# Converting weights through a PSUM bank on VectorE, and placing the second batch's key sums over several blocks

## The chip, the cores and the metric

The kernel runs on one core of a Trainium2 chip. The core has five engines with a queue each: TensorE (PE, matmuls; its weight loads are shown as PEld), VectorE (DVE), ScalarE (ACT), GpSimd (POOL) and SyncE (SP, which issues the DMAs). The metric is the device time of one execution in microseconds: 2738.78 us before the change, the median of three runs (2738.58 to 2742.02).

## The reference

Inputs are q (2 batches of 12288 rows of 128), kv (2 x 384 x 32 x 128), a 128 x 128 projection w_sr, and two pairs of feed-forward weights, 128 x 2048 and 2048 x 128, all float32.

```python
kv_pool = kv.reshape(B, H // 4, 4, W // 4, 4, C).mean(axis=(2, 4))
k = v = kv_pool.reshape(B, -1, C) @ w_sr          # 768 keys a batch
a = softmax(q @ k.T / sqrt(C));  x = a @ v
h = x @ w_in1;  x = (h * clip(h + 3, 0, 6) / 6) @ w_out1
h = x @ w_in2;  out = (h * cos(h)) @ w_out2
```

## The kernel before

**Tiling.** The 24576 rows are cut into 48 blocks of 512, 24 to a batch. A block goes through attention (transposed q, four score tiles of 128 rows by 768 keys, row maximum, exponential, normalisation, transposition of the weights, product with the values) and then through layer 1 and layer 2 in 8 units each. A unit is six matmuls into a pair of PSUM banks (`ff_in`, lines 762 to 764), ScalarE and VectorE work on the pair (lines 777 and 780 in layer 1; 785, 788, 794 and 797 in layer 2), a split of the result into a high and a low part (ScalarE line 824, GpSimd line 800) and six matmuls into an accumulating bank (`ff_out`, lines 770 to 772). Every product is made of three matmuls with operands split into a high and a low part, so the weights have to be split too. Layer 2 runs 15 units behind layer 1.

**Key sums.** `plan_kv` averages 16 rows of kv into a key. A batch has six chunks; a chunk is loaded into two `w` tiles and added up by halves on VectorE (line 445): 1024 elements of one tile to the other, then 512, 256 and 128 within the tile. The first batch stops after two such additions and lets PE finish (`KV_HALVINGS`), the second makes all four. PE transposes the sum (line 454), `mean` copies it into the tile `pt` (line 467), and `project` makes keys and values of it (lines 515, 519, 497, 500).

**Weights.** `plan_weight` converts the 16 parts of the four weight matrices (512 words of 8 bytes a partition each). Its steps use the loaded tile `raw` and a second `w` tile of two halves: `magnitude` (ACT, line 352), `clamp`, `rebase`, `sign` (DVE, lines 357, 364, 371), `high` (ACT, line 390), `power`, `rest` (DVE, lines 378, 385), `low` and `add` (POOL, lines 394, 398). PE may use a part when its last step is done.

**Order.** `Plan.run` writes the order of all engines when the program is built. It is a list scheduler: an operation has a priority in nanoseconds, a cost on the engines that can do it (`where`), operations that it follows, and slots that it takes and gives back (13 `w` tiles, 8 PSUM banks taken singly or as adjacent pairs, and others). Nothing whose priority lies more than `WINDOW` = 100000 above that of the first unfinished operation may begin. `KV_AHEAD` and `KV_PROJECT` say by how much the priority of a batch's key sums and of its projection lies before that of its first block, and the step (2000) how far the six chunks lie apart. On the chip each engine then takes its list strictly in order, and waits where an input or a buffer is not ready.

**PSUM.** Scores, transposed attention weights and each unit's `ff_in` take a pair of the 8 banks; each layer's accumulator, the attention product and small transposes take a single one.

## Time and profile before

| | |
|---|---|
| median of the runs | 2738.78 us |
| profiled execution | 2738.04 us, of which the span is 2736.2 us |
| PE busy | 2649.4 us (97%), 11504 instructions |
| ACT busy | 2308.1 us (84%) |
| DVE busy | 2123.9 us (78%) |
| POOL busy | 2057.3 us (75%) |
| granted PE clock | 0.99 of full speed as a mean |

The busy shares are means over the whole span. The kernel has three regimes: a start, in which keys and weights are prepared; a long stretch in which one block follows the other; and, near 1160 to 1400 us, the change from the first batch to the second. The profile's view by stretches and the timeline show them apart. PE busy means that a matmul is under way, not that PE runs at its full rate, so the time from one block to the next is the better measure of what PE loses.

### The profile page before, as it was taken

The numbers are of one execution on the slowest core, as the hardware profiler recorded it, in microseconds if no ns is written. First come the engines' busy times: TensorE is split into PE (matmuls) and PEld (weight loads), VectorE is DVE, ScalarE is ACT, GpSimd is POOL, SyncE is SP. The second block draws the span as 40 slices with busy tenths as digits, with TensorE's granted clock in tenths as the row PEclk, the third lists the DMA queues.
The fourth block names the chain that finished last, engine by engine and source line by source line (L and its number), as shares of the span: only waits on it lengthen the run. The fifth ranks groups of instructions, "written<-read, shape, count | busy, mean of one in ns | idle before, by whom it ended". The sixth has DMA issues, their size and how long they took to land. (4 is left out here: it accounts for less than half of the span.)

```text
span 2736.2 us, 32247 instructions
## 1 busy us (share of the span) xinstructions
PE 2649.4 (97%) x11504; PEld 2108.1 (77%) x11504; DVE 2123.9 (78%) x2224; ACT 2308.1 (84%) x2647; POOL 2057.3 (75%) x999
## 2 busy tenths in 40 slices
PE   6789999999999999988999999999999999999999
PEld 5567788878877887766788788878877887888787
DVE  6887777777787787788787777877877777778776
ACT  3578888889898888877788898988888888888888
POOL 3786778777777877767687787778777878787777
PEclk9999999999999999999999999999999999999999
DMA  5123222322232232323223222322332232223210
GB/s 174 46 76 82 67 59 71 84 62 55 72 83 62 55 85 70 101 76 85 55 77 77 58 58 72 83 62 55 79 76 62 60 86 68 58 64 90 55 51 12
DMA packets 387058, 193.00 MB, mean 71 GB/s; under 512 B 292561, under 2 KB 367441, under 8 KB 386897
## 3 DMA queue, kind: packets, MB, share of 16 engines
q1 hardware_dynamic: 386896, 190.95, 26.8%
q8 instruction: 90, 1.47, 0.2%
q14 instruction: 72, 0.58, 0.1%
HBM read 33.62 MB, written 84.93 MB: 43 GB/s over the span
## 5 line engine op out<-in xcount | busy, mean ns | idle before, releaser
L800 POOL TENSOR_TENSOR lo<-w,hi 128x1024 fp32r<-128x1024 f32 x768 | 1838.0, 2417 | 609.5 <-ACT hi L824 393.6
L824 ACT CAST hi<-w 128x1024 fp32r<-128x1024 f32 x768 | 786.7, 1056 | 158.9 <-DVE w L780 106.7
L762 PE MATMUL banks<-x,w_in_hi 128*128 128x512 f32 x1536 | 640.0, 417 | 28.1 <-DVE w L780 15.0
L797 DVE TENSOR_TENSOR w<-w,banks 128x1024 f32<-128x1024 f32 x384 | 463.6, 1218 | 206.6 <-ACT w L794 206.5
L770 PE MATMUL banks<-hi,w_out_hi 128*128 128x512 f32 x1536 | 607.4, 395 | 0.0
L764 PE MATMUL banks<-x,w_in_hi 128*128 128x512 f32 x1536 | 603.1, 393 | 1.2 <-DVE x L734 1.2
L763 PE MATMUL banks<-x,w_in_lo 128*128 128x512 f32 x1536 | 602.9, 392 | 0.0
L772 PE MATMUL banks<-lo,w_out_hi 128*128 128x512 f32 x1536 | 600.6, 391 | 1.6 <-POOL lo L800 1.6
L771 PE MATMUL banks<-hi,w_out_lo 128*128 128x512 f32 x1536 | 599.7, 390 | 0.0
L780 DVE SCALAR_TENSOR_TENSOR w<-w,banks 128x1024 f32<-128x1024 f32 x384 | 457.3, 1215 | 138.9 <-ACT w L777 138.8
L788 DVE SCALAR_TENSOR_TENSOR w<-banks,w 128x1024 f32<-128x1024 f32 x384 | 463.7, 1218 | 58.5 <-ACT w L785 56.4
L777 ACT ACTIVATE w<-banks,three 128x1024 f32<-128x1024 f32 x384 | 417.6, 1115 | 57.5 <-PE banks L764 55.0
L794 ACT ACTIVATE w<-w 128x1024 f32<-128x1024 f32 x384 | 404.5, 1067 | 32.8 <-DVE w L788 30.0
L785 ACT ACTIVATE w<-banks 128x1024 int32<-128x1024 f32 x384 | 388.7, 1026 | 49.1 <-PE banks L764 48.2
L762 PEld LDWEIGHTS banks<-x,w_in_hi 128*128 128x128 f32 x1536 | 290.4, 189 | 125.9 <-DVE w L780 27.8
L763 PEld LDWEIGHTS banks<-x,w_in_lo 128*128 128x128 f32 x1536 | 290.6, 189 | 71.4 <-issue 16.5
L764 PEld LDWEIGHTS banks<-x,w_in_hi 128*128 128x128 f32 x1536 | 290.2, 189 | 64.2 <-DVE x L734 1.9
L772 PEld LDWEIGHTS banks<-lo,w_out_hi 128*128 128x128 f32 x1536 | 288.8, 188 | 64.2 <-POOL lo L800 3.1
L771 PEld LDWEIGHTS banks<-hi,w_out_lo 128*128 128x128 f32 x1536 | 289.4, 188 | 60.4 <-issue 2.4
L770 PEld LDWEIGHTS banks<-hi,w_out_hi 128*128 128x128 f32 x1536 | 289.6, 189 | 59.7 <-issue 1.7
L652 DVE COPY w<-w 128x1536 uint16<-128x1536 uint16 x184 | 317.2, 1744 | 1.4 <-POOL w L624 1.1
L711 PE MATMUL banks<-w,v_all 128*128 128x512 f32 x576 | 272.1, 596 | 4.4 <-ACT w L322 2.5
(64 smaller groups left out, 1970.2 us busy)
## 6 DMA issues: line engine op xcount, KB each, us to landing
scr<-w SPq DMA_DIRECT2D x184, 384.0 KB, 2.5
w<-in_kv_dram SPq DMA_DIRECT2D x48, 256.0 KB, 5.9
w<-in_q_dram SPq DMA_DIRECT2D x48, 256.0 KB, 2.8
out_dram<-w SPq DMA_DIRECT2D x48, 256.0 KB, 2.0
w<-in_moe_w_in_dram SPq DMA_DIRECT2D x8, 512.0 KB, 5.4
w<-in_moe_w_out_dram SPq DMA_DIRECT2D x8, 512.0 KB, 4.0
w<-scr SPq DMA_TRANSPOSE x138, 4.6
w_sr_sb<-in_w_sr_dram SPq DMA_DIRECT2D x1, 64.0 KB, 2.0
```

The costliest lines, as they stand in the source:

```text
L762: nc.tensor.matmul(t[:, i, :], w_hi[:, k, :], xx[:, 0, :], start=True, stop=False)
L763: nc.tensor.matmul(t[:, i, :], w_lo[:, k, :], xx[:, 0, :], start=False, stop=False)
L764: nc.tensor.matmul(t[:, i, :], w_hi[:, k, :], xx[:, 1, :], start=False, stop=True)
L770: nc.tensor.matmul(t, o_hi[:, k, :], h[:, i, :], start=(k == 0), stop=False)
L771: nc.tensor.matmul(t, o_lo[:, k, :], h[:, i, :], start=False, stop=False)
L772: nc.tensor.matmul(t, o_hi[:, k, :], l[:, i, :], start=False, stop=(k == 2 * NP - 1))
L777: nc.scalar.activation(plan[g], two(ps), AF.Relu, bias=three, scale=1.0)
L780: nc.vector.scalar_tensor_tensor(out=plan[g], in0=plan[g], scalar=6.0, in1=two(ps), op0=ALU.min, op1=ALU.mult)
L788: nc.vector.scalar_tensor_tensor(out=plan[g], in0=two(ps), scalar=0.25, in1=plan[g].bitcast(I32), op0=ALU.add, op1=ALU.subtract,)
L797: nc.vector.tensor_tensor(out=plan[g], in0=plan[g], in1=two(ps), op=ALU.mult)
L800: nc.gpsimd.tensor_tensor(out=plan[lo], in0=plan[g], in1=plan[hi].bitcast(F32), op=ALU.subtract)
L824: prio + HI_AT, {"act": 947}, lambda e: nc.scalar.copy(plan[hi], plan[g]), [a],
```

## The change

In `plan_weight` the second work tile becomes one PSUM bank (`one(tt)`), and a new slot `turn`, of which there is one, lets one part be converted at a time. The two GpSimd steps go to VectorE: `add` now comes before `low` and adds the rest to the rounded word in PSUM, and `low` subtracts the high part from it. `sign` writes in place into `raw`. A part has seven VectorE instructions in place of five, all with a PSUM operand, and no GpSimd instruction: 112 instead of 80 on VectorE, 32 fewer on GpSimd. The costs that the planner is told change with that. For the key sums `KV_AHEAD` becomes 200000 for both batches; the second batch's chunks lie 25000 apart instead of 2000; `KV_PROJECT` becomes 10000; and the planner is told 1.6 ns for an element of the second batch's additions instead of 1.04.

```diff
--- before.py
+++ after.py
@@ -41,6 +41,8 @@
 BY_PE = 2
 
 NBANKS = 8
+
+TURNS = 1
 ET_SPARE = 2
 
 W_SPARE = 3
@@ -49,7 +51,7 @@
 
 WINDOW = 100000.0
 LOAD_AHEAD = 5000
-KV_AHEAD, KV_PROJECT = 60000, 4000
+KV_AHEAD, KV_STEP, KV_PROJECT = 200000, 25000, 10000
 KV_HALVINGS = 2
 WARM = 3
 A_STEP = 2000
@@ -293,6 +295,7 @@
             "lo": tiles("lo", NLO, [P, 2, T], F32R),
             "x": tiles("x", NX, [P, 2, T], F32R),
             "s": tiles("s", 8, [P, 4], F32),
+            "turn": list(range(TURNS)),
             "one": free_banks,
             "two": free_banks,
             "scr": tiles("scr", NSCR, [NKC // 2, NJ * P * 2, 2 * P], U16, dram),
@@ -340,8 +343,8 @@
             return r[:, :, 0].bitcast(U32), r[:, :, 1]
 
         def work():
-            t = plan[tt].bitcast(I32)
-            return t[:, 0, :], t[:, 1, :]
+
+            return one(tt).bitcast(I32)
 
         def load(e):
             nc.sync.dma_start(
@@ -349,64 +352,64 @@
             )
 
         def magnitude(e):
-            nc.scalar.activation(work()[0].bitcast(F32), words()[1].bitcast(F32), AF.Abs)
+            nc.scalar.activation(work().bitcast(F32), words()[1].bitcast(F32), AF.Abs)
 
         def clamp(e):
 
-            t32 = work()[0].bitcast(F32)
+            t32 = work().bitcast(F32)
             nc.vector.tensor_scalar(
                 out=t32, in0=t32, scalar1=SMALLEST, scalar2=None, op0=ALU.max
             )
 
         def rebase(e):
 
-            t = work()[0]
+            t = work()
             nc.vector.tensor_scalar(
                 out=t, in0=t, scalar1=3, scalar2=0x3FFFFFF8,
                 op0=ALU.logical_shift_left, op1=ALU.bitwise_and,
             )
 
         def sign(e):
-            t, top = work()
+            top = words()[1]
             nc.vector.scalar_tensor_tensor(
-                out=top, in0=words()[1], scalar=-(1 << 30), in1=t,
+                out=top, in0=top, scalar=-(1 << 30), in1=work(),
                 op0=ALU.bitwise_and, op1=ALU.bitwise_or,
             )
 
         def power(e):
-            t, top = work()
             nc.vector.tensor_scalar(
-                out=t, in0=top, scalar1=-(1 << 23), scalar2=None, op0=ALU.bitwise_and
+                out=work(), in0=words()[1], scalar1=-(1 << 23), scalar2=None, op0=ALU.bitwise_and
             )
 
         def rest(e):
 
-            t32 = work()[0].bitcast(F32)
+            t32 = work().bitcast(F32)
             nc.vector.scalar_tensor_tensor(
                 out=t32, in0=words()[0], scalar=2.0**-52, in1=t32, op0=ALU.mult, op1=ALU.mult
             )
 
         def high(e):
-            nc.scalar.copy(hi, work()[1].bitcast(F32))
+            nc.scalar.copy(hi, words()[1].bitcast(F32))
+
+        def add(e):
+            t32 = work().bitcast(F32)
+            nc.vector.tensor_tensor(out=t32, in0=t32, in1=words()[1].bitcast(F32), op=ALU.add)
 
         def low(e):
-            top32 = work()[1].bitcast(F32)
-            nc.gpsimd.tensor_tensor(out=top32, in0=top32, in1=hi.bitcast(F32), op=ALU.subtract)
-
-        def add(e):
-            t, top = work()
-            nc.gpsimd.tensor_tensor(out=lo, in0=top.bitcast(F32), in1=t.bitcast(F32), op=ALU.add)
+            nc.vector.tensor_tensor(
+                out=lo, in0=work().bitcast(F32), in1=hi.bitcast(F32), op=ALU.subtract
+            )
 
         a = op(prio, {"dma": 1560}, load, take=[(raw, "w")], spare=W_SPARE)
-        a = op(prio, {"act": 520}, magnitude, [a], take=[(tt, "w")])
-        a = op(prio, {"dve": 335}, clamp, [a])
-        a = op(prio, {"dve": 335}, rebase, [a])
+        a = op(prio, {"act": 560}, magnitude, [a], take=[(tt, "one"), (("turn", n, part), "turn")])
+        a = op(prio, {"dve": 602}, clamp, [a])
+        a = op(prio, {"dve": 602}, rebase, [a])
         c = op(prio, {"dve": 602}, sign, [a])
         a = op(prio, {"act": 520}, high, [c])
-        c = op(prio, {"dve": 335}, power, [c])
-        a = op(prio, {"pool": 1225}, low, [a, c])
-        c = op(prio, {"dve": 602}, rest, [c], drop=[raw])
-        a = op(prio, {"pool": 1225}, add, [a, c], drop=[tt])
+        c = op(prio, {"dve": 602}, power, [c])
+        c = op(prio, {"dve": 602}, rest, [c])
+        c = op(prio, {"dve": 602}, add, [c, a], drop=[raw])
+        a = op(prio, {"dve": 602}, low, [c], drop=[tt, ("turn", n, part)])
         for k in range(part * WK, (part + 1) * WK):
             w_ready[n, k] = a
 
@@ -472,7 +475,7 @@
             a = [load(0), load(1)]
             for n in range(halvings):
                 w = 1024 >> n
-                where = {"dve": 70 + 1.04 * w}
+                where = {"dve": 70 + (1.6 if b else 1.04) * w}
                 if n == 0:
                     where["pool"] = 2303
                 a = [op(prio, where, add(n), a, drop=[] if n else [keys[1]])]
@@ -893,7 +896,8 @@
     projects = {}
 
     def pool_kv(prio, batch):
-        projects[batch] = plan_kv(prio, batch, 2000, *((4, 0) if batch else (KV_HALVINGS, WARM)))
+        step, *how = (KV_STEP, 4, 0) if batch else (2000, KV_HALVINGS, WARM)
+        projects[batch] = plan_kv(prio, batch, step, *how)
 
     def project_kv(prio, batch):
         for h in range(2):
```

In the changed kernel's rows below, lines above 410 stand 3 higher than before (L445 is L448, L454 is L457, L515 is L518).

PE's queue at the start, the first batch's keys, before. L454 transposes a chunk's sum, L462 is filler, L515 and L519 are the projection of one half, L555 transposes a block's q:

```order
L454 MATMUL banks<-ident,w_82 128x128 x4
L462 MATMUL banks<-ident 128x128 x3
L515 MATMUL banks<-w_84,w_sr_sb 128x384
L519 MATMUL banks<-w_sr_sb,w_84 128x128 x3
L454 MATMUL banks<-ident,w_85 128x128 x4
L462 MATMUL banks<-ident 128x128 x3
L454 MATMUL banks<-ident,w_87 128x128 x4
L462 MATMUL banks<-ident 128x128 x3
L555 MATMUL banks<-ident,w_79 128x128 x4
L454 MATMUL banks<-ident,w_89 128x128 x4
L555 MATMUL banks<-ident,w_78 128x128 x4
```

and in the changed kernel:

```order
L457 MATMUL banks<-ident,w_82 128x128 x4
L465 MATMUL banks<-ident 128x128 x3
L457 MATMUL banks<-ident,w_85 128x128 x4
L465 MATMUL banks<-ident 128x128 x3
L457 MATMUL banks<-ident,w_87 128x128 x4
L465 MATMUL banks<-ident 128x128 x3
L457 MATMUL banks<-ident,w_89 128x128 x4
L465 MATMUL banks<-ident 128x128 x3
L518 MATMUL banks<-w_84,w_sr_sb 128x384
L522 MATMUL banks<-w_sr_sb,w_84 128x128 x3
L518 MATMUL banks<-w_84,w_sr_sb 128x384
L522 MATMUL banks<-w_sr_sb,w_84 128x128 x3
```

The projection of the first half stood after the third chunk; both halves now stand after the sixth, and both transposes of q after them.

ScalarE's queue a little later, before: L352 is `magnitude`, L390 `high`, L609 the exponential, L322 the copy of transposed attention weights:

```order
L352 ACTIVATE w_85<-w_80 128x512
L497 ACTIVATE v_all<-banks 128x384
L352 ACTIVATE w_87<-w_83 128x512
L390 CAST w_in_hi<-w_82 128x512
L352 ACTIVATE w_79<-w_86 128x512
L609 ACTIVATE w_89,s_110<-banks,s_110 128x768
L609 ACTIVATE w_78,s_111<-banks,s_111 128x768
L352 ACTIVATE w_84<-w_88 128x512
L609 ACTIVATE w_81,s_112<-banks,s_112 128x768
L352 ACTIVATE w_82<-w_90 128x512
L390 CAST w_in_hi<-w_85 128x512
```

and in the changed kernel (L355, L392, L612, L325), where L730 is the copy that makes the first block's input of layer 1:

```order
L392 CAST w_in_hi<-w_81 128x512
L612 ACTIVATE w_84,s_114<-banks,s_114 128x768
L612 ACTIVATE w_79,s_115<-banks,s_115 128x768
L325 COPY w_78<-banks 128x1024
L355 ACTIVATE banks<-w_80 128x512
L325 COPY w_81<-banks 128x1024
L325 COPY w_86<-banks 128x1024
L612 ACTIVATE w_88,s_116<-banks,s_116 128x768
L392 CAST w_in_hi<-w_80 128x512
L612 ACTIVATE w_90,s_117<-banks,s_117 128x768
L355 ACTIVATE banks<-w_83 128x512
L730 CAST x_106<-banks 128x512
```

Where several `magnitude` ran ahead, each now writes a bank, `banks`, and comes after the part before it has been finished; one of them stands right ahead of L730.

VectorE's queue where the second batch's key sums begin, before (L445 the additions, L780 the gate of layer 1, L603 the row maximum):

```order
L780 SCALAR_TENSOR_TENSOR w_90<-w_90,banks 128x1024
L445 TENSOR_TENSOR w_79<-w_79,w_80 128x1024
L445 TENSOR_TENSOR w_78<-w_78,w_82 128x1024
L445 TENSOR_TENSOR w_79<-w_79 128x512
L780 SCALAR_TENSOR_TENSOR w_83<-w_83,banks 128x1024
L780 SCALAR_TENSOR_TENSOR w_87<-w_87,banks 128x1024
L780 SCALAR_TENSOR_TENSOR w_88<-w_88,banks 128x1024
L603 TENSOR_REDUCE s_114<-banks 128x1
L603 TENSOR_REDUCE s_115<-banks 128x1
L445 TENSOR_TENSOR w_79<-w_79 128x256
L603 TENSOR_REDUCE s_116<-banks 128x1
L445 TENSOR_TENSOR w_79<-w_79 128x128
```

and in the changed kernel (L448, L783, L800, L791, L564):

```order
L737 TENSOR_TENSOR x_109<-banks,x_109 128x512
L448 TENSOR_TENSOR w_90<-w_90,w_81 128x1024
L564 TENSOR_TENSOR x_104<-banks,x_104 128x512
L791 SCALAR_TENSOR_TENSOR w_82<-banks,w_82 128x1024
L448 TENSOR_TENSOR w_90<-w_90 128x512
L783 SCALAR_TENSOR_TENSOR w_78<-w_78,banks 128x1024
L800 TENSOR_TENSOR w_82<-w_82,banks 128x1024
L783 SCALAR_TENSOR_TENSOR w_88<-w_88,banks 128x1024
L448 TENSOR_TENSOR w_90<-w_90 128x256
L448 TENSOR_TENSOR w_90<-w_90 128x128
L783 SCALAR_TENSOR_TENSOR w_85<-w_85,banks 128x1024
```

The additions of two chunks stood back to back; now those of a chunk stand between the work of units, and the first two chunks begin some 100 rows earlier in VectorE's queue. 22 of the 24 additions remain on VectorE; two first additions (1024 elements) are now in GpSimd's queue.

## Rows read from the trace of the kernel before

**Rows 1.** Stretches of the span: length, busy us of each engine (instructions), PE clock, DMA.
```profile
30.00:60.00 30.00, 19.32 (x86) 15.72 (x85) 29.61 (x50) 17.72 (x33) 19.49 (x16) 0.85 0.23 78
...
60.00:110.00 50.00, 38.34 (x142) 25.54 (x141) 35.48 (x42) 29.96 (x36) 35.43 (x21) 0.92 0.28 84
...
110.00:160.00 50.00, 36.44 (x144) 27.95 (x143) 49.83 (x52) 28.88 (x37) 36.45 (x20) 0.93 0.29 74
...
148.00:284.00 136.00, 124.90 (x516) 96.02 (x516) 107.39 (x109) 110.14 (x126) 102.70 (x52) 0.97 0.30 73
...
400.00:600.00 200.00, 200.00 (x883) 161.66 (x882) 155.68 (x165) 176.61 (x202) 154.48 (x75) 1.00 0.29 72
...
1160.00:1240.00 80.00, 64.36 (x256) 50.78 (x256) 72.15 (x63) 54.25 (x61) 53.65 (x24) 0.88 0.29 75
```

**Rows 2.** ScalarE's timeline: start, us; the layer-2 input cast, once per block.
```profile
389.62 0.61 ACT L729 ACTIVATE x<-banks 128x512 fp32r<-128x512 f32 x1
...
1145.39 0.61 ACT L729 ACTIVATE x<-banks 128x512 fp32r<-128x512 f32 x1
...
1725.06 0.63 ACT L729 ACTIVATE x<-banks 128x512 fp32r<-128x512 f32 x1
```

**Rows 3.** Timeline where the second batch's key sums begin: start, us, [idle before <-releaser].
```profile
1159.38 9.03 POOL L800 TENSOR_TENSOR lo<-w,hi 128x1024 fp32r<-128x1024 f32 x3 [4.08 <-ACT hi L824]
...
1159.79 6.42 DVE L445 TENSOR_TENSOR w<-w,w 128x1024 f32<-128x1024 f32 x2
...
1166.14 2.82 DVE L445 TENSOR_TENSOR w<-w 128x512 f32<-128x512 f32 x1
...
1170.15 1.01 PE L597 MATMUL banks<-k_hi,x 128*128 128x384 f32 x2 [5.39 <-DVE w L780]
```

**Rows 4.** VectorE's groups, 1150 to 1360 us: the second batch's key sums by shape.
```profile
L445 DVE TENSOR_TENSOR w<-w,w 128x1024 f32<-128x1024 f32 x6 | 13.4, 2253 | 0.0
L445 DVE TENSOR_TENSOR w<-w 128x512 f32<-128x512 f32 x6 | 11.1, 1847 | 0.1
L445 DVE TENSOR_TENSOR w<-w 128x256 f32<-128x256 f32 x6 | 9.0, 1508 | 0.0
L445 DVE TENSOR_TENSOR w<-w 128x128 f32<-128x128 f32 x6 | 7.7, 1276 | 0.1
```

**Rows 5.** The page's groups kept apart by shape: weight conversion on VectorE, whole span.
```profile
L385 DVE SCALAR_TENSOR_TENSOR w<-w,w 128x512 f32<-128x512 uint32 x16 | 22.4, 1400 | 0.1
L357 DVE TENSOR_SCALAR w<-w 128x512 f32<-128x512 f32 x16 | 17.4, 1091 | 4.3 <-ACT w L352 4.3
L371 DVE SCALAR_TENSOR_TENSOR w<-w,w 128x512 int32<-128x512 int32 x16 | 15.2, 953 | 0.2 <-PE banks L764 0.2
L364 DVE TENSOR_SCALAR w<-w 128x512 int32<-128x512 int32 x16 | 14.7, 922 | 0.1
L378 DVE TENSOR_SCALAR w<-w 128x512 int32<-128x512 int32 x16 | 10.8, 676 | 0.1
```

**Rows 6.** Single lines of the weight conversion: ns min/median/max.
```profile
L357 DVE TENSOR_SCALAR w<-w x16: 406/428/2601, 30.8 to 165.7; 128x512 f32<-128x512 f32 x16
...
L385 DVE SCALAR_TENSOR_TENSOR w<-w,w x16: 673/1752/2253, 35.4 to 173.4; 128x512 f32<-128x512 uint32 x16
```

**Rows 7.** Groups by shape: VectorE's tensor_scalar of 512 elements that reads PSUM.
```profile
L849 DVE TENSOR_SCALAR w<-banks 128x512 f32<-128x512 f32 x42 | 28.6, 682 | 1.0 <-PE banks L772 0.9
```

**Rows 8.** Timeline of the start: first batch's projection, first scores, first layer-2 unit.
```profile
30.00 0.81 PE L515 MATMUL banks<-w,w_sr_sb 128*128 128x384 f32 x2
30.65 0.83 PE L519 MATMUL banks<-w_sr_sb,w 128*128 128x128 f32 x6
31.23 0.42 PE L597 MATMUL banks<-k_hi,x 128*128 128x384 f32 x1
...
148.25 1.21 DVE L788 SCALAR_TENSOR_TENSOR w<-banks,w 128x1024 f32<-128x1024 f32 x1
```

**Rows 9.** SyncE's issues of the second batch's key loads: ns min/median/max.
```profile
L433 SPq DMA_DIRECT2D w<-in_kv_dram x24: 536/565/600, 1149.9 to 1275.4; - x24
```

## The prediction

> **What bounds the kernel now.** I read the view by stretches first, then the timeline of one instruction that comes once per block, then the timeline where that period breaks. Between 400 and 600 us PE is busy for 200.00 of 200 us at full clock while VectorE has 155.68, or 78% [rows 1]: there only PE's own work counts. The layer-2 input cast comes once per block, 48 times in all. From 389.62 to 1145.39 lie 14 periods, 53.98 us each; the ten from 1145.39 to 1725.06 take 579.67 us, where ten full-rate periods would take 539.8 [rows 2]. So the change of batch costs 39.9 us, and in the first 80 us of it (1160 to 1240) PE is busy 64.36 us at a granted clock of 0.88, and VectorE 72.15 [rows 1]. Why is seen in the timeline: three additions stand in a row on VectorE from 1159.79 to 1168.96, 9.2 us, beside a GpSimd that works without a gap; the gate behind them is late, and PE waits 5.39 us for its bank [rows 3]. PE had thus about 3.8 us of work in hand. The four shapes of addition average 2.25, 1.85, 1.51 and 1.28 us, with little fall for an eighth of the elements [rows 4]: much of it is waiting for GpSimd.
>
> The other loss is the start. VectorE is busy 29.61 of 30 us to 60, 35.48 of 50 to 110, 49.83 of 50 to 160, and PE falls behind [rows 1]. There the 80 conversion instructions take 22.4 + 17.4 + 15.2 + 14.7 + 10.8 = 80.5 us, 1.006 us each [rows 5], though the same shapes take 0.406 or 0.673 us at best [rows 6]: 48 x 0.406 + 32 x 0.673 = 41.0 us is work, 39.5 us is waiting. Two things are therefore worth time: VectorE's at the start and in the middle. GpSimd's relief is worth only what it takes from VectorE.
>
> **The start.** Each part has seven VectorE steps for five, 112 for 80. None has two inputs in SBUF, and all touch PSUM. The nearest row is the tensor_scalar of the same size that reads PSUM, 0.682 us [rows 7]; no row writes PSUM from VectorE. Bounds: 0.406 (the fast SBUF form) to 1.006 (today's mean with its waits), 45 to 113 us for all. I take 0.682, being the same shape with a PSUM operand: 76.4 us. So VectorE's total falls by only 4.1 us: the two moved steps and the three that go from 0.406 to 0.682 eat the 39.5 us of waiting.
>
> What matters more is when it falls due. Up to the first layer-2 unit, which starts at 148.25 [rows 8], VectorE's queue holds the same units, row maxima and halves in both kernels, but 68 conversion instructions before and 66 after: 68 x 1.006 = 68.4 us against 45.0, a gain of 23.4. After it come 46 x 0.682 = 31.4 us where 12 x 1.006 = 12.1 stood, 19.3 more. Against the gain stands the projection: its first half ran while PE waited for chunks; now both follow the sixth. One half costs PE about 1.5 us (0.81 and 0.83, overlapping) [rows 8], the two transposes of q with their casts now follow it rather than lie beside the loads, about 3 us more: the first scores start at some 35.7 instead of 31.23, 4.5 us late. ScalarE's queue gets a new wait: each `magnitude` waits for the part before, and behind the third stands the cast of the first block's layer-1 input. Following the three queues with the durations above, that input still comes some 5 us sooner than before, since 16 conversion steps stand ahead of it in VectorE's queue (10.9 us) where 30 did.
>
> So the first layer-2 unit comes about 23.4 - 4.5 = 18.9 us earlier if VectorE idles there as it does now (15 us from 30 to 160 [rows 1]). Then the 19.3 us of late conversions have to fit where VectorE idles 28.6 of 136 us (148 to 284) and PE is already busy 124.90 [rows 1]. If all fits, the start gains 18.9 us; if none, it loses 0.4. Idle time of that share is partly latency between engines, so I take less than half, 8 us.
>
> GpSimd loses 32 instructions; it idles in this stretch as it is, and I count nothing for it.
>
> **The middle.** The order now knows the additions at 1.6 ns an element, so it puts other work between them. 22 stay on VectorE; at today's durations 4 x 2.25 + 6 x (1.85 + 1.51 + 1.28) = 36.8 us; two first additions go to GpSimd, which has room. In VectorE's queue they lie in three groups: 11 additions among 57 instructions (18.4 us), 4 among 10 (6.9), 7 among 22 (11.5). VectorE does 165 instructions in 200 us with 22% slack [rows 1], so the other 46, 6 and 15 instructions bring 12.4, 1.6 and 4.0 us of slack. Backlogs of 6.0, 5.3 and 7.5 us less the 3.8 us that PE has in hand leave 2.2 + 1.5 + 3.7 = 7.4 us lost. PE's own matmuls for keys and values and the hand-over to the new keys stay; I put these at 8 us. Loss 15.4 of 39.9: gain 24.5.
>
> The other reckoning is by share. From the first of these additions to the last are 140 other instructions, 170 us at full rate, with 132 us of VectorE work; with 36.8 that is 169. If VectorE can be no busier than the 72.15 of 80 it reached [rows 1], this takes 187 us: 17 lost, and 8: gain 15. I take 21. Fewer PE waits should also hold the clock at full speed, which is in these numbers.
>
> The 24 loads of the second batch, 0.565 us of SyncE's queue each [rows 9], move some 115 us forward, past stores and q loads that are not urgent; SyncE has room for 13.6 us there, and if a load holds up q, at most its own 0.6 us is late. The tile `pt` is held longer, one `w` tile of 13; its price is nothing while units find tiles, and I keep 5 us for it in the range.
>
> The Trainium skill ("SBUF — State Buffer", on the port pair that VectorE and GpSimd share) says that whichever instruction starts first keeps the pair to its end and the other is blocked for that long. By that rule spreading takes no waiting away, since each addition still meets GpSimd at work; the trace agrees that the smallest addition averages 1.28 us. This is the third rival below, whose price is worked out there from rows.
>
> **Sum.** 8 + 21 = 29 us off the profiled 2738.04 gives 2709 us. The median of the runs, 2738.78, is 0.7 us from the profiled execution, which I neglect. A difference of 0.2% (5.5 us) is what a measurement of this kernel can tell from none.
>
> **Rivals.**
> 1. The start gains nothing: the late conversions push units back, 2738 - 21 = 2717, and with the middle at 15 and the start 5 us worse, 2728. For it: the total on VectorE falls by only 4.1 us. Against: VectorE idle time there. Chance 0.20.
> 2. Both ends come: the start 18.9, the middle up to 30, as backlogs stay under 3.8 us: 2689. Chance 0.14.
> 3. The additions wait as long as ever and the loss only moves 100 us forward. At 36.8 us against 41.2 (13.4 + 11.1 + 9.0 + 7.7 [rows 4]) it keeps nine tenths, 36 of 39.9; the start then decides: 2726 with 8 us gained, 2735 with none. For it: additions hardly shorten with their size. Against: no run of additions is longer than 6.1 us, where it was 9.2. Chance 0.08.
> 4. Slower: the missing bank. From the first layer-2 unit to the last conversion both accumulators and the conversion hold three banks, so two pairs are left, where there were three. A full-rate unit has 53.98 / 16 = 3.37 us; two pairs allow a unit every half holding time. Above 6.75 us of holding they become the bound; over 120 us, 36 units, a mean of 9 us costs 36 x 1.13 = 41 us, and with the middle's gain of 21 the kernel takes 2758. It is slower from about 8 us on. For it: layer 2 uses a pair in five steps, and VectorE will be nearly full. Against: the conversions hold their bank only part of that time. Chance 0.06.
>
> The forecast has 0.52: its own range is 2698 to 2722. The 80% range leaves out the fourth case and the end of the second: 2692 to 2733. Faster takes the forecast, rivals 1 and 2 and most of 3: 0.90; the rest of 3 is the same, 0.04; slower 0.06.
>
> **What would show it.** In the changed profile: conversion steps near 0.68 us with little spread (right), or above 1 (the start's step wrong); the first layer-2 unit near 130 to 140 us, with about 8 us of that lead left once the conversions end; first scores near 35.7; no PE wait above 3 us at the additions, VectorE 90 to 97% busy around them; the period's excess at the change of batch 15 to 25 us. A period of 54 us throughout the earlier blocks and an unchanged excess at the change would speak for rival 3, PE waits for a bank between 140 and 270 us for rival 4.

## The result, and where the time came from

The changed kernel takes 2715.52 us as a median of four runs (2709.69 to 2716.63), the kernel before 2738.68 beside it: a ratio of 0.9909, 95% interval 0.9892 to 0.9927. It is 23.2 us faster, and 2709 was forecast. The sum came out near for a reason that the forecast did not give: the start gained far more than its 8 us, the middle far less than its 21.

The profiled execution takes 2709.69 us, of which the span is 2707.6; it is the fastest of the four. Two casts that come once per block part the gain. The first fence is of the kernel before, the second of the changed kernel; each has the cast of the seventeenth block, the last that comes before the second batch's sums do any harm, and that of the twenty-ninth, the first after it (start, us).

```profile
982.93 0.63 ACT L729 ACTIVATE x<-banks 128x512 fp32r<-128x512 f32 x1
...
1671.59 0.61 ACT L729 ACTIVATE x<-banks 128x512 fp32r<-128x512 f32 x1
```

```profile
962.16 0.61 ACT L732 ACTIVATE x<-banks 128x512 fp32r<-128x512 f32 x1
...
1643.04 0.62 ACT L732 ACTIVATE x<-banks 128x512 fp32r<-128x512 f32 x1
```

Up to the first of them the changed kernel is 20.8 us ahead; that is the start. Between them lie twelve periods, 688.66 us before and 680.88 after. At 53.98 us each [rows 2] they would take 647.8, so the change of batch costs 40.9 us before and 33.1 after: a gain of 7.8. What follows takes the same time in both. A second profile of the changed kernel, of an execution of 2715.85 us that stands near the median, splits the gain in the same way, though with less of it:

```profile
966.69 0.63 ACT L732 ACTIVATE x<-banks 128x512 fp32r<-128x512 f32 x1
...
1648.90 0.62 ACT L732 ACTIVATE x<-banks 128x512 fp32r<-128x512 f32 x1
```

There the start is 16.2 us ahead and the excess 34.4, a gain of 6.5. The two numbers, the start (this first cast) and the excess over twelve periods, are used for every kernel below.

**The start.** The view by stretches of the changed kernel, columns as in [rows 1]:

```profile
30.00:60.00 30.00, 26.82 (x148) 21.15 (x149) 23.93 (x48) 20.03 (x36) 7.15 (x8) 1.00 0.23 84
60.00:110.00 50.00, 42.56 (x173) 31.22 (x171) 47.45 (x64) 39.03 (x47) 31.23 (x15) 0.97 0.28 97
110.00:160.00 50.00, 44.14 (x172) 31.24 (x173) 49.10 (x62) 41.14 (x49) 28.11 (x13) 1.00 0.35 88
148.00:284.00 136.00, 128.69 (x548) 100.52 (x548) 116.84 (x139) 116.45 (x136) 97.54 (x48) 0.99 0.23 61
...
1000.00:1080.00 80.00, 70.28 (x299) 55.37 (x298) 65.98 (x61) 63.56 (x72) 53.47 (x25) 0.96 0.39 100
```

Against [rows 1], PE does 148 matmuls from 30 to 60 us where it did 86, and 172 from 110 to 160 where it did 144. From 148 to 284 VectorE is busy 116.84 us where it was 107.39: it takes in the late conversions, and PE is still busier than before. The conversion by shape (engine, operation, tiles, count, busy us, mean ns), and one line with its shortest, median and longest instruction:

```profile
L367 DVE TENSOR_SCALAR banks<-banks 128x512 int32<-128x512 int32 x16 | 11.1, 696 | 0.3
L360 DVE TENSOR_SCALAR banks<-banks 128x512 f32<-128x512 f32 x16 | 11.1, 694 | 2.3 <-ACT banks L355 2.3
L396 DVE TENSOR_TENSOR banks<-banks,w 128x512 f32<-128x512 f32 x16 | 11.1, 694 | 0.2
...
L374 DVE SCALAR_TENSOR_TENSOR w<-w,banks 128x512 int32<-128x512 int32 x16 | 10.9, 684 | 0.2
...
L399 DVE TENSOR_TENSOR w_out_lo<-banks,w_out_hi 128x512 fp32r<-128x512 f32 x8 | 5.5, 684 | 0.2
```

```profile
L360 DVE TENSOR_SCALAR banks<-banks x16: 687/692/705, 37.9 to 216.4; 128x512 f32<-128x512 f32 x16
```

All seven steps last 0.69 us and together 77.3 us; the same line ran from 406 to 2601 ns before [rows 6]. The longest of all 112 instructions takes 0.705 us: the waiting is gone, not only smaller. The first scores and the first layer-2 unit:

```profile
35.66 0.61 PE L600 MATMUL banks<-k_hi,x 128*128 128x384 f32 x2 [0.24 <-ACT x L561]
...
124.39 1.23 DVE L791 SCALAR_TENSOR_TENSOR w<-banks,w 128x1024 f32<-128x1024 f32 x1 [0.52 <-ACT w L788]
```

Scores begin 4.4 us later than before, the layer-2 unit 23.9 us earlier [rows 8], and of those 23.9 us 20.8 are left at the seventeenth block. From 30 us to that unit VectorE is busy 85.05 us where it was 103.17, and idle 9.3 us where it was 15.1: 18.1 us of the lead are work that it no longer has there, 5.7 are idle time.

**The middle.** VectorE's additions of the second batch (900 to 1300 us), by shape, in the changed kernel:

```profile
L448 DVE TENSOR_TENSOR w<-w 128x256 f32<-128x256 f32 x6 | 10.7, 1784 | 0.1
L448 DVE TENSOR_TENSOR w<-w 128x128 f32<-128x128 f32 x6 | 10.3, 1716 | 0.1
L448 DVE TENSOR_TENSOR w<-w 128x512 f32<-128x512 f32 x6 | 9.5, 1589 | 0.0
L448 DVE TENSOR_TENSOR w<-w,w 128x1024 f32<-128x1024 f32 x4 | 8.0, 1996 | 0.7 <-issue 0.6
```

The 22 take 38.5 us, where 24 took 41.2 [rows 4]; the two smallest shapes have even grown, from 1.51 and 1.28 us to 1.78 and 1.72. An eighth of the elements costs nearly as much as the whole. What GpSimd does beside them decides it, as single additions show:

```profile
1005.59 0.68 DVE L448 TENSOR_TENSOR w<-w 128x512 f32<-128x512 f32 x1
...
1007.57 4.87 POOL L803 TENSOR_TENSOR lo<-w,hi 128x1024 fp32r<-128x1024 f32 x2 [7.84 <-ACT hi L827]
1007.72 2.51 DVE L448 TENSOR_TENSOR w<-w 128x256 f32<-128x256 f32 x1
...
1172.37 0.28 DVE L448 TENSOR_TENSOR w<-w 128x128 f32<-128x128 f32 x1
```

The first begins when GpSimd has been idle for 5.9 us, and takes 0.68 us for 512 elements; the second begins just after a GpSimd instruction has begun, and takes 2.51 for 256; the third lies between two GpSimd instructions (1168.52 to 1170.92, and from 1173.02) and takes 0.28 for 128. The timeline where three of them stand in a row (start, length, [idle before <- releaser]):

```profile
1036.27 7.64 POOL L803 TENSOR_TENSOR lo<-w,hi 128x1024 fp32r<-128x1024 f32 x3 [0.66 <-ACT hi L827]
...
1036.71 7.35 DVE L448 TENSOR_TENSOR w<-w 128x512 f32<-128x512 f32 x3
...
1045.25 0.79 PE L773 MATMUL banks<-hi,w_out_hi 128*128 128x512 f32 x1 [5.77 <-DVE w L783]
...
1045.84 0.63 PE L774 MATMUL banks<-hi,w_out_lo 128*128 128x512 f32 x1
...
1049.27 0.40 PE L774 MATMUL banks<-hi,w_out_lo 128*128 128x512 f32 x1
```

The three additions end with GpSimd's three instructions, one behind each: 512, 256 and 128 elements take 2.51, 2.46 and 2.32 us, and GpSimd's instructions 2.40, 2.80 and 2.52. The gate behind them is late, and PE waits 5.77 us, longer than the 5.39 of [rows 3]; its first matmuls after it take 0.63 us instead of 0.39. PE's waits from 962 to 1643 us, grouped (engine, tile, line <- what it waited for: us, times, longest):

```profile
PE banks L457 <- DVE w L448: 6.4, 2, 3.3
PE banks L773 <- DVE w L783: 5.8, 1, 5.8
PE banks L765 <- DVE w L800: 3.3, 2, 2.4
```

A second kind of wait is on top: L457 is PE's transposition of a sum. It stands in PE's queue between the matmuls of units, so that all units behind it wait for the last addition of a chunk. These waits are most of the excess, but not all of it. The same twelve periods in the changed kernel, and in the version below whose additions all run on GpSimd in the old order (2681.07 us; columns as in [rows 1]):

```profile
962.00:1643.00 681.00, 661.83 (x2862) 524.80 (x2861) 539.43 (x550) 576.69 (x661) 509.46 (x243) 0.99 0.29 73
```

```profile
961.00:1616.00 655.00, 654.35 (x2863) 521.44 (x2862) 505.28 (x532) 575.29 (x661) 529.68 (x265) 1.00 0.30 78
```

PE is idle 19.2 us in the first and 0.6 in the second, and the same matmuls keep it busy 7.5 us longer, at a granted clock of 0.99 against 1.00.

### The profile page after: what moved, and what is told of

Read it like the earlier page. It is cut to its first block, busy times and chain, and to the rows that moved or that the text cites. A ratio compares the mean times of both kernels' runs of the same rounds, so it can differ in the third digit from the quotient of the medians.

```text
span 2707.6 us, 32274 instructions
## 1 busy us (share of the span) xinstructions
PE 2641.4 (98%) x11504; PEld 2100.2 (78%) x11504; DVE 2115.5 (78%) x2254; ACT 2310.1 (85%) x2647; POOL 2010.5 (74%) x969
## 5 line engine op out<-in xcount | busy, mean ns | idle before, releaser
L800 DVE TENSOR_TENSOR w<-w,banks 128x1024 f32<-128x1024 f32 x384 | 463.6, 1217 | 198.9 <-ACT w L797 198.6
L783 DVE SCALAR_TENSOR_TENSOR w<-w,banks 128x1024 f32<-128x1024 f32 x384 | 457.8, 1214 | 116.9 <-ACT w L780 116.1
L791 DVE SCALAR_TENSOR_TENSOR w<-banks,w 128x1024 f32<-128x1024 f32 x384 | 463.7, 1217 | 60.1 <-ACT w L788 58.1
L780 ACT ACTIVATE w<-banks,three 128x1024 f32<-128x1024 f32 x384 | 418.1, 1115 | 55.8 <-PE banks L767 52.6
L797 ACT ACTIVATE w<-w 128x1024 f32<-128x1024 f32 x384 | 404.4, 1067 | 35.8 <-DVE w L791 33.1
L766 PEld LDWEIGHTS banks<-x,w_in_lo 128*128 128x128 f32 x1536 | 289.5, 188 | 71.1 <-issue 15.1
```

Of the source, the lines that this page charges most:

```text
L766: nc.tensor.matmul(t[:, i, :], w_lo[:, k, :], xx[:, 0, :], start=False, stop=False)
L780: nc.scalar.activation(plan[g], two(ps), AF.Relu, bias=three, scale=1.0)
L783: nc.vector.scalar_tensor_tensor(out=plan[g], in0=plan[g], scalar=6.0, in1=two(ps), op0=ALU.min, op1=ALU.mult)
L791: nc.vector.scalar_tensor_tensor(out=plan[g], in0=two(ps), scalar=0.25, in1=plan[g].bitcast(I32), op0=ALU.add, op1=ALU.subtract,)
L800: nc.vector.tensor_tensor(out=plan[g], in0=plan[g], in1=two(ps), op=ALU.mult)
```

## Experiments

The theory: GpSimd is busy three quarters of the time (509.46 of 681 us above), and a VectorE instruction with both inputs in SBUF waits for the GpSimd instruction that is under way. So did the steps with one input in SBUF and their output there too (L357, up to 2601 ns [rows 6]). The conversion gains because its steps no longer meet that; the additions lose in the middle because they still do. Rivals are named with each run. The diffs show the core of each edit against the changed kernel; nothing else differs in the source, but the planner may then order neighbouring work a little differently.

**One part of the change alone.** First the weights:

```diff
-KV_AHEAD, KV_STEP, KV_PROJECT = 200000, 25000, 10000
+KV_AHEAD, KV_STEP, KV_PROJECT = 60000, 2000, 4000
-                where = {"dve": 70 + (1.6 if b else 1.04) * w}
+                where = {"dve": 70 + 1.04 * w}
```

> The new weight conversion alone; the key sums of both batches planned as before. Theory A (the change is two independent gains, about 21 us at the start from the conversion and 7 us at the change of batch): about 2717 us, 21 us under the kernel before, block 20's layer-2 cast some 21 us earlier than before, and the excess of the change of batch back at about 40 us. Theory B (the conversion is worth the 8 us of the prediction, and the rest of the start's gain comes from the earlier key sums of the first batch): about 2731 us.

Then the key sums alone, with `plan_weight` as in the kernel before; its core:

```diff
-            return one(tt).bitcast(I32)
+            t = plan[tt].bitcast(I32)
+            return t[:, 0, :], t[:, 1, :]
...
-            nc.vector.tensor_tensor(
-                out=lo, in0=work().bitcast(F32), in1=hi.bitcast(F32), op=ALU.subtract
-            )
+            top32 = work()[1].bitcast(F32)
+            nc.gpsimd.tensor_tensor(out=top32, in0=top32, in1=hi.bitcast(F32), op=ALU.subtract)
```

> The spread key sums alone (priorities, step, cost of an addition); the weights converted as before, with GpSimd. Theory A: the excess at the change of batch goes from 40 to about 33 us, and the start loses up to 4 us by the later projection: 2732 to 2736 us. Theory B (the spreading is worth 21 us as predicted, and the changed kernel's profile happened to be a bad one there): about 2718 us.

The conversion alone takes 2709.92 us (ratio 0.9895, 0.9880 to 0.9910): start 957.43, 25.5 us ahead of before, excess 37.4. That is 7 us better than theory A, since both parts are, and far from B. PE's waits in the middle are those of before, almost to the tenth of a microsecond; the first two groups of this kernel (957 to 1643 us), then of the kernel before (983 to 1672):

```profile
PE banks L600 <- DVE w L783: 11.1, 2, 5.7
PE banks L765 <- DVE w L783: 6.1, 7, 2.0
```

```profile
PE banks L597 <- DVE w L780: 11.1, 2, 5.7
PE banks L762 <- DVE w L780: 6.1, 7, 2.0
```

That the same waits cost 37.4 and not 40.9 us goes with a mean granted clock of 0.99 against 0.98 in that stretch; why the clock differs stays open. The key sums alone take 2730.72 us (0.9971, 0.9960 to 0.9982): start 988.00, 5.1 us late, excess 27.9, 13.0 less, where theory A had 7 and the prediction 21. So the whole change, at 2715.52, is no better than the conversion alone.

**Where the order of the key sums loses.** The first batch's lead was set back to its old value and the second batch's kept; the changed kernel ran again on the same chip.

```diff
-                work.append((t - KV_AHEAD, 0, lambda pr, batch=batch: pool_kv(pr, batch)))
+                work.append((t - (KV_AHEAD if batch else 60000), 0, lambda pr, batch=batch: pool_kv(pr, batch)))
```

> The changed kernel, but the first batch's key sums are planned with the old lead of 60000, so that its first half is projected after the third chunk again; the second batch keeps 200000. Theory A (the later projection costs the start about 5 us, as the two kernels with one half of the change show): block 17's layer-2 cast some 5 us earlier than in the changed kernel, 957 us, and with the excess of the changed kernel's profile (33 us) 2704 to 2711 us. Theory E (the place of the projection is hidden under the conversion, and the 5 us come from elsewhere): no difference, 2710 to 2716 us.

> The changed kernel itself, again, on the chip of the other three, since its four runs (2709.69 to 2716.63) spread more than the others' do, and its profile was of the fastest. Theory A: a median of 2713 to 2717 us, with a granted clock of 0.993 to 0.996, so that it is 3 to 7 us slower than the kernel with the conversion alone. Theory G (the first runs were on a slower chip): 2709 to 2711 us.

With the old lead for the first batch: 2702.29 us (0.9863, 0.9847 to 0.9878), start 957.42, excess 29.9. The changed kernel again: 2713.56 (0.9901, 0.9887 to 0.9914), start 966.69, excess 34.4. The start loses 4.7 to 9.3 us to the longer lead of the first batch's sums, where I expected 5, and the middle 3 to 4 more. The second batch's additions take 34.1 us on VectorE in the first of these kernels and 38.5 in the other, since the planner gives GpSimd three first additions there and two here; that this is the reason is not shown. Without that lead the two parts do nearly add up: 25.5 in the start and 11.0 in the middle.

**Is it the place of the conversion's work tile?** The turn and the seven VectorE steps stay, but the working words go back into a `w` tile.

```diff
-            return one(tt).bitcast(I32)
+            return plan[tt][:, 0, :].bitcast(I32)
-        ... take=[(tt, "one"), (("turn", n, part), "turn")])
+        ... take=[(tt, "w"), (("turn", n, part), "turn")])
```

> The changed kernel, but the bank that holds the work of a weight part is a tile in SBUF again; the seven steps on VectorE, their order and the one turn stay. Theory P (the start is won because operands in PSUM keep the steps from waiting for GpSimd): the steps that took 0.69 us take 1.0 to 1.5 us as a mean with maxima above 2 us, VectorE's conversion is 112 to 160 us instead of 77, and the kernel takes 2735 to 2775 us. Theory O (the start is won by the new order and by GpSimd's 32 instructions, not by the bank): the single-source steps fall to 0.41 us, the conversion takes 63 to 75 us, and the kernel 2700 to 2716 us.

It takes 2758.64 us (1.0064, 1.0052 to 1.0077): 0.6% slower than before, 45.1 us slower than the changed kernel beside it. Its conversion by shape:

```profile
L396 DVE TENSOR_TENSOR w<-w,w 128x512 f32<-128x512 f32 x16 | 19.7, 1230 | 0.3
...
L360 DVE TENSOR_SCALAR w<-w 128x512 f32<-128x512 f32 x16 | 12.4, 772 | 0.6 <-ACT w L355 0.6
...
L399 DVE TENSOR_TENSOR w_out_lo<-w,w_out_hi 128x512 fp32r<-128x512 f32 x8 | 11.3, 1407 | 0.3
```

```profile
L396 DVE TENSOR_TENSOR w<-w,w x16: 677/692/2782, 48.0 to 219.2; 128x512 f32<-128x512 f32 x16
```

The eight groups sum to 104.1 us instead of 77.3. The median of L396 is 0.692, but some of its instructions take up to 2.78 us: those wait. So do the steps with one SBUF input; L360, with a median of 0.422, takes up to 2.62 us. The first layer-2 unit starts at 152.37 us, 25.5 to 28 us later than in the two profiles of the changed kernel (126.83 and 124.39). By then VectorE has spent 62.5 us on conversion (72 steps) where the changed kernel had spent 45.3 (66 steps), so 17 us of the delay are longer conversion; what the rest is stays open. The excess is 34.5, as there. At the seventeenth block it is 42 us late (1008.68 against 966.69); the 14 to 16.5 us on top come with a granted clock of 0.85 from 148 to 284 us, where the changed kernel's two profiles had 0.99 and 0.96:

```profile
148.00:284.00 136.00, 107.96 (x397) 79.83 (x397) 114.53 (x121) 92.44 (x109) 75.17 (x35) 0.85 0.15 37
```

So with one turn and the new order of the key sums, moving the two GpSimd steps to VectorE is a loss without the bank; the bank makes it a gain. VectorE's conversion is 27 us longer without it; what the extra `w` tile costs, one of 13, this run does not separate.

**Fewer small additions, or none on VectorE.** Three kernels change the second batch's sums. One stops after two additions and lets PE sum four pieces:

```diff
-        step, *how = (KV_STEP, 4, 0) if batch else (2000, KV_HALVINGS, WARM)
+        step, *how = (KV_STEP, 2, 0) if batch else (2000, KV_HALVINGS, WARM)
```

> The changed kernel, but the second batch's chunks stop after two additions (1024 and 512 elements), as the first batch's do, and TensorE sums the remaining four pieces: 12 short additions leave VectorE, 18 matmuls of 128 columns come to TensorE. Theory A (what is left of the excess is additions that each wait for a GpSimd instruction, whatever their size: 12 of them took 21 us of VectorE): the excess falls from 33 to about 15 us, 2699 us. Theory C (the excess is TensorE's own wait for the sums, the hand-over to the new keys and the w tiles held longer): no gain, 2715 to 2719 us.

It takes 2698.05 us (0.9853, 0.9840 to 0.9867), start 965.11, excess 18.6, near theory A's 15, though a third first addition also went to GpSimd. The next puts all four additions on GpSimd, and the third does so with the old lead and step:

```diff
-                where = {"dve": 70 + (1.6 if b else 1.04) * w}
-                if n == 0:
+                where = {"dve": 70 + 1.04 * w}
+                if b:
+                    where = {"pool": 130 + 2.25 * w}
+                elif n == 0:
```

> The changed kernel, but all four additions of the second batch's chunks run on GpSimd, so that they never meet a GpSimd instruction on the other engine. Theory A: VectorE is rid of 38 us of additions, GpSimd gets about 5 us a chunk and has room; the excess falls to 12 to 18 us, about 2697 us. Theory D (GpSimd's split results come late behind the additions and hold up TensorE): the excess stays at 33 us or grows, 2715 us or more.

> All four additions of the second batch's chunks on GpSimd, as in the earlier run of that kind, but with the lead, the step and the lead of the projection as before the change (60000, 2000, 4000): not spread. Theory A (the excess at the change of batch is VectorE's waiting, and spreading is not needed once the additions are off VectorE): excess 8 to 12 us, the start 5 us earlier: 2681 to 2690 us. Theory F (GpSimd can take the additions only when they are spread: six chunks in a row are some 27 us ahead of the split results): excess 20 to 35 us, 2695 to 2708 us.

They take 2685.83 (0.9808, 0.9794 to 0.9821) and 2681.07 us (0.9781, 0.9768 to 0.9795), with an excess of 7.7 and 7.3, lower than theory A in both. The start is at 962.86 and 961.11: the old lead brought 1.8 us there, not the 5 that I expected. On GpSimd the small additions get shorter with their size, as they did not on VectorE (the first of these kernels, 900 to 1300 us):

```profile
L448 POOL TENSOR_TENSOR w<-w 128x512 f32<-128x512 f32 x6 | 7.9, 1311 | 0.0
...
L448 POOL TENSOR_TENSOR w<-w 128x256 f32<-128x256 f32 x6 | 4.5, 748 | 0.1
L448 POOL TENSOR_TENSOR w<-w 128x128 f32<-128x128 f32 x6 | 2.8, 465 | 0.2
```

The only group of PE's waits over 0.1 us in the twelve periods of the second (961 to 1616 us):

```profile
PE banks L767 <- DVE w L802: 0.5, 2, 0.3
```

With the additions off VectorE, their spreading brings nothing to the excess, and 7.3 us is what is left; with PE busy 654.35 of 655 us, I take it for PE's own work on the keys. This version is the fastest of the study.

**The small additions out of PSUM.** This run tells the waiting from the mere presence of the additions: they stay on VectorE, spread as in the changed kernel, but the 512-element addition writes a bank, and one reduction out of that bank replaces the two small ones.

```diff
+                    to = one(sums) if b and n else f
                     ENG[e].tensor_tensor(
-                        out=f[:, 0:w], in0=f[:, 0:w], in1=f2[:, at : at + w], op=ALU.add
+                        out=to[:, 0:w], in0=f[:, 0:w], in1=f2[:, at : at + w], op=ALU.add
...
+            def four(e):
+                nc.vector.tensor_reduce(
+                    out=flat(plan[keys[0]])[:, 0:C],
+                    in_=one(sums).rearrange("p (e c) -> p c e", c=C), op=ALU.add,
+                    axis=mybir.AxisListType.X,
+                )
```

> The changed kernel, but of each chunk of the second batch the 512-element addition writes a PSUM bank and one reduction of 512 elements out of that bank takes the place of the 256- and 128-element additions; the priorities, the spreading and the costs of the first two additions are those of the changed kernel. In the changed kernel these 12 small additions took 10.7 + 10.3 = 21.0 us of VectorE; six reductions out of PSUM, by the row maximum's 0.95 us for 768 elements, should take about 0.7 us each, 4.2 us. Theory A (what the change of batch still loses is VectorE waiting for GpSimd inside additions with both inputs in SBUF): some 17 us of VectorE time go, and the excess over twelve blocks falls from 33 to 34 us to 17 to 24: 2697 to 2705 us, and the reductions show little spread. Theory B (the additions' place in the order and PE's own wait for each sum set the loss, not the waiting inside them): PE waits for the sums as before, excess 29 to 34, 2709 to 2716 us.

It takes 2693.17 us (0.9831, 0.9817 to 0.9844), start 963.22, excess 16.7. Its sums on VectorE and GpSimd (900 to 1300 us), and PE's longest waits from 963 to 1628 us:

```profile
L450 DVE TENSOR_TENSOR banks<-w 128x512 f32<-128x512 f32 x6 | 11.3, 1876 | 1.0 <-POOL w L450 0.9
L457 DVE TENSOR_REDUCE w<-banks 128x128 f32<-128x512 f32 x6 | 4.1, 683 | 0.1
```

```profile
L450 POOL TENSOR_TENSOR w<-w,w 128x1024 f32<-128x1024 f32 x4 | 10.1, 2524 | 0.4 <-DMA w<-in_kv_dram 0.4
```

```profile
PE banks L778 <- DVE w L796: 2.1, 3, 1.3
PE banks L613 <- DVE w L796: 1.8, 2, 1.4
```

The reduction of 512 elements out of the bank takes 0.683 us; the addition that writes the bank but still reads twice from SBUF takes 1.88 as a mean. For an addition with two SBUF inputs it is the inputs, then, not the output, that make it wait. PE waits at most 1.4 us at a time and no longer for a sum. The result is 4 us better than the low end of what I expected, for which there is a second reason: the planner gave GpSimd four first additions here, not two. How much of the gain is that reason's, this run does not tell.

**Two turns.** Two parts in conversion at once, on the fastest version:

```diff
-TURNS = 1
+TURNS = 2
```

> The version with the second batch's additions on GpSimd and the old lead and step (2681.07 us), with two turns in place of one, so that two weight parts can be in conversion and two banks are held. Theory A (the start waits for the chain of one part: magnitude, seven steps, and the wait of the next magnitude): VectorE's idle time before 110 us goes, the start shortens by 4 to 8 us, 2673 to 2678 us. Theory B (VectorE's own time sets the start, it is busy 48 of 50 us from 60 to 110 us already): no difference, 2678 to 2684 us. Theory C (the second bank leaves the units too few pairs): slower, 2685 to 2700 us, with PE waiting for a bank in the first 280 us.

It takes 2684.46 us (0.9795, 0.9782 to 0.9808), not to be told from 2681.07, whose interval overlaps. Theory A is out. The first layer-2 input cast comes at 108.0 instead of 123.0 us, but the first layer-2 unit at 130.07 instead of 128.64, with 85 conversion steps ahead of it on VectorE instead of 68, and at the seventeenth block no lead is left (963.4 against 961.1). PE waits 13.0 us for layer 1's gate where it waited 4.9 (30 to 290 us):

```profile
PE banks L767 <- DVE w L785: 13.0, 7, 5.3
```

Whether that is VectorE's time or the second bank is not settled.

## Why the prediction was right, and which steps of it failed

The sign and the mechanism of the start held, and the time lies in the range: 2715.52 us where 2709 was forecast. Two terms of the sum were mis-sized in opposite directions. In the first profile the start brought 20.8 us instead of 8 and the middle 7.8 instead of 21, 28.6 together where 29 was forecast; in the second profile 16.2 and 6.5, together 22.7, near the 23.2 of the medians. That the sum fits is luck.

**Conversion steps at 0.682 us: right.** Measured 0.69 with hardly any spread, 77.3 us for 76.4. Total VectorE time fell as little as forecast, and the start gained all the same, because what counts is what falls due before the first layer-2 unit: 23.9 us earlier, where the full reckoning had 18.9. Not every part of that reckoning held. The 68 and 66 steps, counted rightly, took 64.7 and 45.3 us, 19.4 less and not 23.4; but VectorE idles 5.7 us less there, which the reckoning had left as it was.

**"I take less than half, 8 us": wrong.** This is the step that failed at the start. I held that VectorE's idle time from 148 to 284 us was partly latency and could not take in the late conversions. It took in what came: busy 116.84 of 136 us, and PE was still busier than before, 128.69 against 124.90 us. Alone, the conversion keeps 25.5 us. The idle time was usable; that steps of constant length made it so is my reading, which no run tests. I had a reckoning from rows and halved it by a guess.

**First scores 35.7 us, 4.5 us late: right,** at 35.66 in the first profile; in the second it is 38.09, and the conversion alone, with the old order of projection, has 33.77, so that the start of the scores is uncertain by some 2.5 us from one execution to the next. Its price was about right too: 4.7 us between the first profile and the kernel with the old lead (9.3 with the second), 5.1 by the key sums alone.

**36.8 us for the additions, at the durations before: right in sum (38.5), wrong in use.** I took a run of at most 6.1 us and turned runs into backlog with VectorE's 22% slack. Three in a row took 7.35 us, because a row of short additions lines up with GpSimd's queue, one GpSimd instruction each. The planner was told 1.6 ns an element, 0.27 us for 128 elements that took 1.72; small additions stand in a row in its order, as things that it took for cheap. And I left out PE's own wait for a sum, 6.4 us: its transposition stands in an in-order queue. Instead of 7.4 us lost to backlog and 8 us of PE's own work, it was 25.8 and 7.3: this is the step that failed in the middle. Of the 25.8, 18.6 are PE's waits, and about 7 go with the clock after them, which the prediction took to be at full speed. The 8 was right, as the version on GpSimd shows.

**VectorE 90 to 97% busy around the additions: wrong.** It was busy 65.98 of 80 us, 82%, from 1000 to 1080 us; PE's losses came from single late instructions, not from a full engine. The reckoning by share was therefore the wrong model too.

**Rivals.** The third, that the additions wait as long as ever, describes the middle: it has 33.1 of 40.9 us left. Its price assumed that the start would gain 8 at most, which is why its times of 2726 and more (2734, not 2735, by its own figures) did not come. I gave it 0.08 and let "no run of additions is longer than 6.1 us" speak against it, which was a number from the same wrong term. The Trainium skill ("SBUF — State Buffer", Who interferes with whom) says that a VectorE instruction with two SBUF inputs contends with GpSimd's reads, and one with at most one SBUF input, outside the two-port modes, does not. The traces agree on both halves: 1.72 us for 128 elements out of SBUF twice, 0.683 for 512 out of the bank. Whether the one-input steps that waited [rows 6] were in such a mode, no run here shows. Rival 1, a start that gains nothing, is refuted by the conversion alone, which keeps 25.5 us of it. Rival 2 had the start nearer, at 18.9. Rival 4, the missing bank, didn't show: from 30 to 300 us PE is busy 246.50 us where it was 226.93, and the bank is what makes the gain.

## What to carry to other kernels

When an engine's instructions wait for those of a busy neighbour, first ask of each where its operands lie: a step with at most one input from SBUF and an operand in PSUM, at a steady 0.69 us, beat one that takes 0.41 us at best and 2.6 at worst. An instruction's price in a planner must be what it takes beside that neighbour, and short ones are then the dearest per element; spreading them took 6 to 13 us off an excess of 41, spreading and other operands together 24, another engine 33. And don't halve a reckoning from rows for caution: write the caution into the range. At the start the reckoning that followed the queue was the nearer one (18.9 against 8); in the middle it was not (24.5, the share gave 15, and 7.8 was measured), and I take the mean durations and the mean slack that went into it for the reason.

## What was not expected of the hardware

Additions of 128 and 256 elements on VectorE last 1.72 and 1.78 us beside GpSimd, longer than those of 512 (1.59), while GpSimd itself does them in 0.47 and 0.75 us. For these sums GpSimd was the cheaper engine. The waiting also goes the other way: an addition of 1024 elements that began first took 1.22 us, and the GpSimd instruction that began during it took 3.31 us, where 2.40 is usual:

```profile
1091.63 1.22 DVE L448 TENSOR_TENSOR w<-w,w 128x1024 f32<-128x1024 f32 x1
1091.81 3.31 POOL L803 TENSOR_TENSOR lo<-w,hi 128x1024 fp32r<-128x1024 f32 x1 [2.23 <-issue]
```

After PE's 5.77 us wait the granted clock from 1045 to 1049 us is 0.53 as a mean, which is near the lower of its two levels (1.2 and 2.4 GHz), and a matmul of 512 columns takes 0.63 us until it is back at 0.39, some 3.6 us after the wait:

```profile
1045.00:1049.00 4.00, 3.75 (x9) 2.99 (x10) 4.00 (x5) 2.27 (x3) 0.59 (x1) 0.53 0.00 0
```
